# RWKV attention and a sentence-level expert layer: attention outputs summed transposed by 64x32 tiles, expert weights in halves, opening reordered

## The chip, the cores and the metric

One core of a Trainium2 chip. The metric is the device time of one launch in microseconds (us). A run is "fast" when it lies within 1.5% of the fastest run of the same kernel, else "slow"; comparisons below are of fast runs unless a sentence says otherwise. In the traces TensorE (PE in the profile, PEld for its weight loads) is granted either the full clock (1.00) or half of it (0.50); for a longer stretch the profile gives the mean.

## The reference

Four sequences of 768 positions, 8 heads of 48 columns. Attention keeps a 48x48 state a head; then each whole sequence is sent to one of 8 experts.

```python
for t in range(S):
    cur = einsum('bhd,bhe->bhde', u[None] * kt, vt)
    y[:, :, t] = einsum('bhd,bhde->bhe', rt, state + cur)
    state = w[None, :, :, None] * state + einsum('bhd,bhe->bhde', kt, vt)
x = y as (B, S, 384)
logits = x.mean(axis=1) @ w_gate            # one expert a sequence
e_idx = argmax(logits); gate_w = softmax(logits)[e_idx]
out = gate_w * (maximum(x @ w1[e_idx], 0) @ w2[e_idx])    # 384 -> 1024 -> 384
```

## The kernel before

The 768 positions of a sequence are three groups of 256, so there are 12 groups. A group is: scaled k and r (`kp`, `rp`), transposes of both, scores in two rounds masked by VectorE (`gt`), then y = scores x v, plus the bonus term u and the carried state. The suffixes `_x`, `_y` and names such as `kp`, `rp`, `vt` (v times the bonus) are tiles and helpers of the kernel; a "mode change" below is TensorE going from matmuls of one tile shape to those of another. `y` comes out with positions on the partitions, so ScalarE evicts it (`xn`), TensorE transposes it back, and ScalarE evicts it again into `xt`, which the expert layer reads. Sequence b's expert jobs (`hp`: 3 matmuls for the first layer; `op`: 4 for half of the second) are let into "slots" of the next sequence's groups, 8.5 a group in seven slots; the first gate must be known before the first job.

```python
def scores_v(g, j, first):                       # cut
    def y_mm(i):                                 # 32 a group: load 64x128, move 48 columns
        h, c = divmod(i, 2); p, a = divmod(h, 2)
        nc.tensor.matmul(out=yj[:, D * h : D * h + D],
            lhsT=gt[q, p // 2, a, p % 2, c, :], rhs=vb[q, c, h, :], ...)
    def s_mm(i):                                 # 16 a group: load 64x128, move 96 columns
        p, c = divmod(i, 2)
        nc.tensor.matmul(out=sp[:, 96 * p : 96 * p + 96],
            lhsT=kp[g % NR][qo, c, 2 * p : 2 * p + 2, :]..., rhs=vb[qo, c, 2 * p : 2 * p + 2, :]..., ...)
    for i in range(H):
        y_mm(2 * i)
        if with_state: s_mm(i)
        y_mm(2 * i + 1)

def add_bonus(g):                                # 4 matmuls a group, 384 columns each
    for j, c in ((0, 0), (1, 1), (0, 1), (1, 0)):
        nc.tensor.matmul(out=ys[g][j][64 * c : 64 * c + 64, 0:DM], lhsT=ident[q, q], rhs=vt[q, c, :], ...)

def backs(g):                                    # 6 transposes, 6 pooling matmuls, one 0.80 us copy
    ...
def mm1(b, w1, ht, ft, sb):
    for ct in range(NCT):
        nc.tensor.matmul(out=hp[:, 0:SB], lhsT=w1[:, ct, ft::NFT], ...)   # step 8 through w1
```

## Time and profile before

| | before |
|---|---|
| time, median of 3 runs (range) | 154.54 us (153.83 to 156.16) |
| span of the profile, mean clock | 152.6 us, 0.978 |
| first gate known; first expert job | 33.3; 45.0 us |
| last gate known | 120.3 us |
| matmuls (each has a weight load beside it) | 1951 |

How to read it: the opening (to 45 us) is a chain of waits; the loop (first job to last gate, 75.3 us) keeps TensorE full (busy 77.4 of the 78.5 us from 45 to 123.5); the tail (32.3 us) is expert jobs alone. The prediction below shows the rows. One view that I passed over belongs here, the DMA queues: queue, kind, packets, MB and share of the DMA engines' time.

```profile
q1 hardware_dynamic: 39460, 18.89, 42.9%
q0 software_dynamic: 1152, 6.29, 22.3%
q8 instruction: 15, 0.25, 0.6%
```

The last line is, by the view's name for it, the program itself on its way to an engine: 15 packets of 16 KB. At 0.6% of the DMA time it looks like nothing, and as bandwidth it is nothing.

### The profile page before, as it was taken

How to read it: one execution, taken by the hardware profiler on the slowest of the kernel's cores; microseconds unless marked ns; L12 is line 12 of the kernel's file. 1: busy time of each engine (PE TensorE's matmuls, PEld its weight loads, DVE VectorE, ACT ScalarE, POOL GpSimd, SP SyncE). 2: the span in 40 equal slices, each digit the busy share in tenths (PEclk: the TensorE clock that was granted, in tenths of full speed). 3: DMA queues.
4: the chain of work that ended last, by engine and by line, in shares of the span. 5: the costliest groups of instructions: out<-in, count | busy, mean ns of one | idle time of the engine just before them, and what ended most of it. 6: DMA issues, size and time to landing. Idle time of an engine off the chain costs nothing.

```text
span 152.6 us, 4539 instructions
## 1 busy us (share of the span) xinstructions
PE 139.5 (91%) x1951; PEld 97.9 (64%) x1951; DVE 74.4 (49%) x164; ACT 83.6 (55%) x144; POOL 68.5 (45%) x62
## 2 busy tenths in 40 slices
PE   6999877956989999999999999999999999999991
PEld 2266645644767878766677877666777765676560
DVE  7837796125465654754548456465562321121110
ACT  0976567351356766546476784563664543556231
POOL 4169659207976839289292862963021020000000
PEclk9999999995599999999999999999999999999999
DMA  2999998303999999999991000998020079960034
GB/s 59 301 322 321 279 268 226 99 0 92 227 215 297 249 312 269 293 214 210 215 376 48 4 0 4 153 195 267 22 93 4 0 111 208 161 247 0 0 126 185
DMA packets 41464, 25.47 MB, mean 167 GB/s; under 512 B 38755, under 2 KB 39012, under 8 KB 41444
## 3 DMA queue, kind: packets, MB, share of 16 engines
q1 hardware_dynamic: 39460, 18.89, 42.9%
q0 software_dynamic: 1152, 6.29, 22.3%
q8 instruction: 15, 0.25, 0.6%
q10 hardware_dynamic: 832, 0.00, 0.3%
q14 instruction: 5, 0.04, 0.1%
HBM read 26.76 MB, written 4.72 MB: 206 GB/s over the span
## 4 chain that ended last, share of the span: by engine, by line
PE 78%; DVE 10%; ACT 8%; issue 2%; DVEq 0%
PE op L503 21%; PE hp L483 21%; PE twp L236 7%; PE at L260 5%; DVE gt L268 5%; PE fill L113 5%; PE y L353 5%; ACT kr L246 4%; PE s L361 2%; PE xp L402 2%; ACT ht L490 2%; PE y L313 2%; PE y L323 2%; DVE ht L492 1%; DVE st L376 1%
## 5 line engine op out<-in xcount | busy, mean ns | idle before, releaser
L483 PE MATMUL hp<-xt,w 128*128 128x384 bf16 x192 | 41.4, 334 | 1.3 <-DVE lg L436 0.3
L503 PE MATMUL op<-w,ht 128*128 128x384 bf16 x192 | 34.9, 326 | 0.1
L246 ACT COPY kr<-twp 128x1024 bf16<-128x1024 bf16 x24 | 24.1, 1011 | 18.4 <-PE twp L236 18.4
L268 DVE TENSOR_TENSOR gt<-at,mask 128x1024 bf16<-128x1024 f32 x24 | 29.3, 1221 | 8.8 <-PE at L260 8.6
L490 ACT ACTIVATE ht<-hp 128x384 bf16<-128x384 f32 x48 | 23.4, 491 | 17.8 <-PE hp L483 17.1
L483 PEld LDWEIGHTS <-w 128*128 128x128 bf16 x192 | 25.0, 148 | 8.1 <-issue 4.4
L305 POOL TENSOR_TENSOR vt<-vb,tcol 128x768 bf16<-128x768 bf16 x11 | 16.3, 1477 | 25.4 <-DVE tcol L297 25.4
L503 PEld LDWEIGHTS <-ht 128*128 128x128 bf16 x192 | 17.3, 97 | 11.1 <-issue 0.8
L247 DVE TENSOR_TENSOR prod<-twp,kr 128x512 bf16<-128x512 bf16 x24 | 10.2, 424 | 27.8 <-ACT kr L246 27.8
L199 POOL TENSOR_TENSOR kp<-k,dk 128x768 bf16<-128x768 f32 x11 | 20.0, 1816 | 1.4 <-DMA k<-in_k_dram 1.4
L199 POOL TENSOR_TENSOR rp<-r,dr 128x768 bf16<-128x768 f32 x11 | 20.0, 1820 | 0.0
L510 ACT ACTIVATE ob<-op,gw 128x384 f32<-128x384 f32 x16 | 9.3, 581 | 13.2 <-PE op L503 12.9
L113 PE MATMUL fill<-zero 128*128 128x512 bf16 (+1 forms) x45 | 14.5, 430 | 1.9 <-DVE zero L85 1.3
L353 PEld LDWEIGHTS <-gt 64*128 64x128 bf16 x384 | 11.5, 94 | 5.0 <-issue 3.9
L492 DVE TENSOR_SCALAR ht<-hp 128x384 bf16<-128x384 f32 x16 | 8.9, 554 | 11.7 <-PE hp L483 11.5
L353 PE MATMUL y<-vb,gt 64*128 64x48 bf16 x384 | 14.1, 182 | 0.4 <-ACT xn L389 0.4
L260 PE MATMUL at<-kr 48*64 48x128 bf16 x384 | 10.5, 229 | 3.6 <-ACT kr L246 1.7
L389 ACT CAST xn<-y 128x384 bf16<-128x384 f32 x24 | 11.1, 480 | 4.1 <-PE y L323 3.5
L462 POOL DMA_DIRECT2D w<-in_moe_w_dram x4 | 2.5, 623 | 22.5 <-DVE gw L452 7.8
L260 PEld LDWEIGHTS <-kr 48*64 48x64 bf16 x384 | 7.0, 110 | 8.2 <-issue 6.2
L410 ACT COPY xt<-xp 128x768 bf16<-128x768 bf16 x12 | 9.6, 798 | 4.3 <-PE xp L402 4.3
L361 PE MATMUL s<-vb,kp 64*128 64x96 bf16 x160 | 10.5, 208 | 0.4 <-DVE st L376 0.4
(73 smaller groups left out, 155.6 us busy)
## 6 DMA issues: line engine op xcount, KB each, us to landing
w<-in_moe_w_dram POOLq DMA_DIRECT2D x8, 768.0 KB, 10.2
k<-in_k_dram SPq DMA_DIRECT2D x12, 384.0 KB, 5.1
r<-in_r_dram SPq DMA_DIRECT2D x12, 384.0 KB, 5.8
v<-in_v_dram SPq DMA_DIRECT2D x12, 384.0 KB, 5.7
out_dram<-ob SPq DMA_DIRECT2D x11, 384.0 KB, 5.6
out_dram<-ob SPq DMA_DIRECT2D x2, 192.0 KB, 1.9
wuT<-in_w_dram ACTq DMA_DIRECT2D x2, 0.8 KB, 3.6
wuT<-in_u_dram ACTq DMA_DIRECT2D x2, 0.8 KB, 4.1
```

Source lines behind the costliest of these rows:

```text
L113: nc.tensor.matmul(out=fills[-1][:, 0:cols], lhsT=zero[:, 0:128], rhs=zero[:, 0:cols], start=True, stop=True)
L199: eng.tensor_mul(dst[:, cs, :, 0:D].rearrange("q c h d -> q h c d"), src[:, :, cs, :], dec[:, :, cs, :])
L246: nc.scalar.copy(kts[g][:, :, :, c, :], tw)
L260: nc.tensor.matmul(out=at[64 * j : 64 * j + 64, a, pp, cs, :], lhsT=kt[q, p, j, cs, :], rhs=rt[q, p, j].rearrange("q c i -> q (c i)"), sta ...
L268: nc.vector.tensor_mul(gts[g][:, rnd].rearrange("q a p c t -> q (a p) c t"), at.rearrange("q a p c t -> q (a p) c t"), mask.rearrange("q n ...
L305: nc.gpsimd.tensor_mul(vt, vbs[g].rearrange("q c h d -> q (c h) d"), tcol.to_broadcast([128, 2 * H, D]))
L353: nc.tensor.matmul(out=yj[:, D * h : D * h + D], lhsT=gt[q, p // 2, a, p % 2, c, :], rhs=vb[q, c, h, :], start=(first and i == 0), stop=(c ...
L361: nc.tensor.matmul(out=sp[:, 96 * p : 96 * p + 96], lhsT=kp[g % NR][qo, c, 2 * p : 2 * p + 2, :].rearrange("s a b -> s (a b)"), rhs=vb[qo, ...
L389: nc.scalar.copy(xns[g][:, j, :], ys[g][j][:, 0:DM])
L483: nc.tensor.matmul(out=hp[:, 0:SB], lhsT=w1[:, ct, ft::NFT], rhs=xts[b][:, ct, SB * sb : SB * sb + SB], start=(ct == 0), stop=(ct == NCT - 1),
L490: nc.scalar.activation(out=o, in_=hp[:, 0:SB], func=ACT.Relu)
L503: nc.tensor.matmul(out=op[:, 0:DM], lhsT=ht[:, ft, 128 * si : 128 * si + 128], rhs=w2[:, ft, :], start=(ft == 0), stop=(ft == NFT - 1),)
```

## The change

Its intent: sum y already transposed (channels on the partitions), so that the two evictions, the back transposes and the pooling matmuls go; pack the sums into 64x32 tiles and scores and state into 64x64 tiles, so that several run side by side (in the trace before, four score matmuls on four 64x64 tiles start within 10 ns, at 89.54 us); fetch each expert's w1 as two halves, whose weight slices step by 4 elements in place of 8; and reorder the opening around a shorter path to the first gate. The core of the diff, cut:

```diff
-    wrow = const.tile([1, DM], FP32, tag="wrow", name="wrow")
-    nc.sync.dma_start(out=wrow, in_=w.rearrange("(o h) d -> o (h d)", o=1))
+    wbc = const.tile([128, DM], FP32, tag="wbc", name="wbc")
+    nc.sync.dma_start(out=wbc, in_=w.rearrange("h d -> (h d)").partition_broadcast(128))
+    load(0, "kr")
+    load(1, "kr")
...
+        def mm(h, c, u):                                   # y: 64 a group, load 64x32, move 128
+            nc.tensor.matmul(
+                out=y_slice(ys[g][j], G), lhsT=vb[q, c, o : o + 32],
+                rhs=gts[g][q, p // 2, a, p % 2, c, :], ...
+        def mm(p, u):                                      # carried state: 32 a group
+            nc.tensor.matmul(
+                out=y_slice(ys[g][j], G), lhsT=sts[g, j][q, p, 32 * u : 32 * u + 32], ...
+        def mm(G, c):                                      # bonus: 48 a group, load 64x32, move 64
+            nc.tensor.matmul(
+                out=y_slice(ys[g][j], G)[:, 64 * c : 64 * c + 64],
+                lhsT=vt[q, c, 32 * G : 32 * G + 32], rhs=ident[q, q], ...
+        def mm(h, c):                                      # state: 32 a group, 64x64
+            nc.tensor.matmul(
+                out=s_ps[g // NB][64 * a : 64 * a + 64, 64 * p : 64 * p + 64],
+                lhsT=kp[g % NR][q, c, h, :], rhs=vb[q, c, window(h) : window(h) + 64], ...
...
+    def part_y(g):
+        together(row0, row1)                # y, bonus, carried state: up to 112 matmuls in turn
+        nc.tensor.drain()
+        together(inter_mms(g, 0, 1), inter_mms(g, 1, 0))
+        together(state_mms(g, 1))
...
-        w1 = wpool.tile([128, NCT, F], BF16, tag="w1", name=f"w1_{b}")
+        for fh in range(2):
+            t = wpool.tile([128, NCT, HF], BF16, tag=f"w1_{fh}", name=f"w1_{b}_{fh}")
...
     gate(0)
     weights(0)
     gate_weight(0)
...
+    bonus(3)
+    prep_k(4)                               # GpSimd's k and r of group 4, now behind the weights
+    prep_r(4)
...
+        slot()
+        acc[1] = True                       # jobs let in from the third slot of group 3, not the sixth
```

## The prediction

> **What bounds the kernel now.** I read the page's engine rows and slices first, then the chain that ended last in order of time, then the groups of instructions.
>
> ```profile
> PE 139.5 (91%) x1951; PEld 97.9 (64%) x1951; DVE 74.4 (49%) x164; ACT 83.6 (55%) x144; POOL 68.5 (45%) x62
> ...
> PE   6999877956989999999999999999999999999991
> ...
> PEclk9999999995599999999999999999999999999999
> ```
>
> TensorE is the only engine near its limit, and the clock row shows where it is not: slices 9 and 10 (34 to 42 us) are half speed. The stretches view says the same in three stages:
>
> ```profile
> 45.00:123.50 78.50, 77.40 (x1217) 58.19 (x1210) 42.57 (x90) 47.98 (x84) 41.07 (x32) 1.00 0.64 160
> 123.50:152.60 29.10, 25.24 (x145) 16.10 (x142) 4.70 (x8) 11.01 (x21) 0.00 (x0) 1.00 0.52 134
> 35.00:45.00 10.00, 8.62 (x168) 6.29 (x167) 5.87 (x9) 3.60 (x6) 9.62 (x8) 0.69 0.88 187
> ```
>
> From 45 to 123.5 us TensorE is busy 77.4 of 78.5 us: nine attention groups and expert jobs share it, and nothing else matters there. Before 45 us the kernel is a chain of waits through all engines; after 123.5 us only expert jobs are left. The chain, at the points that bound the stages:
>
> ```profile
> 33.28 0.18 DVE top L438
> ...
> 35.06 0.67 PE at L260 x12
> ...
> 45.11 0.64 PE hp L483 x3
> ...
> 75.32 0.45 PE twp L236 x8
> ...
> 84.66 0.45 PE twp L236 x8
> ...
> 94.39 0.45 PE twp L236 x8
> ...
> 123.53 7.82 PE op L503 x48
> ...
> 134.45 1.21 PE hp L483 x6
> ```
>
> The first gate is known at 33.3 us, the first expert job runs at 45.1, and one group's transposes return every 9.3 to 9.7 us. The slot rate puts 8.5 expert jobs into a group.
>
> [...]The old w1 slice steps 8 bf16[...]; the new one steps 4[...]. [...]step 8 loads in 148 ns, step 3 in 104, contiguous in 97.
>
> ```profile
> L483 PEld LDWEIGHTS <-w 128*128 128x128 bf16 x192 | 25.0, 148 | 8.1 <-issue 4.4
> L503 PEld LDWEIGHTS <-ht 128*128 128x128 bf16 x192 | 17.3, 97 | 11.1 <-issue 0.8
> ...
> L402 PEld LDWEIGHTS <-xn 128*128 128x128 bf16 x72 | 5.0, 104 | 1.7 <-ACT xn L389 0.9
> ```
>
> [...]The score matmuls show it: four on four 64x64 tiles start within 10 ns, the next four 56 ns later[...].
> [...]The trace has about 0.10 us between the end of one mode's stream and the next mode's first matmul (scores to expert job at 89.80 to 89.89)[...].
>
> **The change part by part, in the steady loop.** From the starts in the trace, one middle group costs TensorE before: transposes 16 x 55.7 ns = 0.89; scores 2 x 0.35 = 0.70; bonus column 0.20; y with state 2 x 0.50 = 1.00; the state's share of y 8 x 66 ns = 0.53; bonus into y 0.29; back transposes 6 x 55.7 = 0.33; pooling 6 x 26 = 0.16; carried state 0.26. Sum 4.36 us. Jobs: an hp job is 3 x 183 ns = 0.55, an op half job 4 x 167 = 0.67, so 16 and 12 of them average 0.60, times 8.5 = 5.1. Together 9.5, which is the period seen.
>
> After, matmuls grow from 1951 to about 3160. I count tiles: a tile is held 56 ns by 128 columns and 29 ns by 64[...], so a run of four that names a tile twice takes two turns. Part x: 16 y matmuls of one row tile in the column order 0,1,3,0 then 1,2,0,1: 0.40. Part y: the longer row has 32 y in the same order (0.79), 24 bonus (0.18) and 8 carried (0.15): 1.1[...]. The drain: last matmul's latency of 0.2[...], 0.3. Behind it 16 matmuls, 0.17. State: 2 x 16 matmuls of 64 columns on two tiles, 0.24 each. Scores stay in the state's mode: 0.25 + 0.25. Transposes 0.89, carried 0.11, bonus column 0.20, logits 6 x 26 ns = 0.16. Mode changes 6 x 0.10 = 0.6. Sum 4.9 us (5.4 with slower issue). So a group costs TensorE 0.55 us more, not less: 64x32 tiles would be cheap if the eight were used evenly, but the order hits one tile twice in four, and 176 matmuls stand where 72 stood. Over eight and a half groups: +4.7 us.
>
> Given back: step-4 weights. In a long stream the 143 ns load hides under 162 ns of matmul; it shows only after short matmuls, where the second hp matmul starts 220 ns after the first instead of 162. That is about 58 ns in some 40 stretches, 2.3 us. In the tail hp jobs run at 0.63 us because two PSUM banks wait for their eviction (0.49 to 0.57), so nothing is gained there. The gate: six fp32 passes of 127 ns become two, 0.5 us at each of three gates in the loop, 1.5 us. ScalarE loses one 0.80 us copy a group, and VectorE some 0.3, but neither is the bound, so that is worth nothing in the loop. Net of the loop: about +1 us.
>
> **The opening.** The w broadcast puts 0.2 MB ahead of the inputs; at about 0.3 MB/us k and r land 0.6 us later, and r set the first transposes before. Gained back: VectorE makes one of the two kr copies, so the first masked scores start at about 11.2 us (11.4 before). Then I walked the new order with the measured durations: vt on VectorE to 15.1, part y of group 0 to 16.75, then st, prod, and scores of group 1 at 17.7 (16.65 before), 19.4; the logits of group 0 wait for the gate constants that GpSimd makes behind a 1.48 us vt, to 21.5; part x, transposes, part y of group 1 to 25.8; scores of group 2 at 26.75 and 28.45 (21.1 and 24.6 before). Here the transposed sum pays: from the last score mask to the gate's logits there are 4.8 us instead of 8.7, without xn, back transposes and pooling. The first gate comes at about 33.2 us, where it is now (33.1).
>
> From the gate to the first job: before, 12 us, in which kp of group 4 was already done. After, GpSimd has weights (1.8), then vt of group 3 (1.48), kp and rp of group 4 (1.82 each) in that order, and vt waits for the bonus column behind exps, vb (0.84), kr (1.01), prod (0.42), the second transposes, kr, prod, and a 1.22 us mask: about 7 us after the gate. So rp of group 4 ends some 12 us after the gate; the transposes of group 4 wait for it, then scores, part x and the second transposes, which wait for a kr copy. First job about 15.5 us after the gate, near 49 us, 4 us later than now, although half of w1 should have landed 7.3 us after the gate (issue at +2.05, first packet 2.8 later, 2.3 for a half). Part y of group 3 and more stands behind it than before (+1.8), while three more slots per the first group take four jobs out of the tail, at nearly no gain.
>
> Sum: 152.6 span +4 (first job) +1.8 (more of group 3 left) +1 (loop) -0.5 (tail) = 158.9 us, and the time is 1.8 above the span: 160.7. I do not take it whole: the walk stacks waits, each of which I may have put too late, and nobody writes a change of this size to lose 6 us. I go to 157.
>
> **Rivals.** First, the opening is shorter: if the waits I stacked overlap and the first job is bound by the half of w1 alone, it starts 7.3 us after a gate at 31 to 33 us, so at 39 to 41, and the loop costs the same: 152.6 - 5 + 1.8 + 0.5 = 150 span, about 151. The halves and the earlier start of the jobs speak for it; the order of GpSimd's work (weights, vt, kp, rp) against. Second, tiles pack better than my count: if the column conflicts cost nothing, part y is 0.6 and a group 4.2 us, 6 us less in all, 147 to 151.[...] Third, issue or the load of 64-column weights becomes the bound[...]: +0.7 us a group, 163 to 166. Fourth, ScalarE was the hidden bound and its saved 0.80 us a group shortens the period: 48 us busy of 78.5 speaks against it.
>
> **Range and chances.** My count says slower, the rivals that mend the opening or the packing say faster, and they are independent of each other. I give 157 us, 148.5 to 165, faster by over 2% (under 151.5) 0.27, within 2% 0.33, slower (over 157.6) 0.40.
>
> **What would show it.** The period of the transposes in the loop: 9.5 to 9.9 if the count is right, under 9 if tiles pack. Part y from first to last matmul: 1.5 to 1.6 us with its drain. The w load at 104 to 110 ns. The first gate at 32 to 35 us and the first hp at 47 to 50; GpSimd's rp as what the transposes of group 4 wait for. A first hp at 40 us would break the sum, and so would a group's attention under 4.3 us.

The sum: 4.9 us for a group, 158.9 us for the span, 160.7 us for the time, taken down to 157. Of the drain's 0.3 us only the 0.2 of a matmul's record is from the trace (state and y records are 0.18 to 0.21); the other 0.1 was the author's assumption. The 5.4 us of a group "with slower issue", and with it the third rival's +0.7, stood on a slower issue rate that no trace had shown. The 29 ns for 64 columns are the author's estimate, between the starts in the trace for 48 columns (25 ns apart, L353) and for 96 (43, L361). That a run of four which names a tile twice takes two turns, and that step 4 loads faster than step 8, were assumptions when they were written (in the changed kernel the last of part x's y matmuls start in pairs 52 to 54 ns apart, 69.57 to 69.74 us); the 104 to 110 ns given for the load lie near the 104 of step 3. Against the second rival the trace has only that y matmuls alone start 26 ns apart (16 from 87.45 us), and y and state matmuls in turn 17 (24 from 85.70).

## The result, and the profile after

The changed kernel is correct and takes **192.66 us** (191.32 to 194.07, 4 fast runs) against 154.56 (153.83 to 156.16, 4 runs). The ratio of fast runs is 1.2486, 95% interval 1.2367 to 1.2605. That is 38 us slower, far outside the range of 148.5 to 165.

Busy rows and clock row of the changed kernel:

```profile
PE 150.5 (78%) x3157; PEld 99.6 (52%) x3159; DVE 71.9 (37%) x154; ACT 72.8 (38%) x126; POOL 75.7 (39%) x75
...
PE   7487449683269699989859689996696998769992
...
PEclk9999655566555999999988978999799999978999
```

TensorE is busy 78% of the span where it was busy 91%, in a kernel that gave it more instructions; no other engine is fuller than before. The clock row has half-speed digits through slices 5 to 13, and dips later, where the kernel before had two. So nothing is a busy bound here: TensorE waits. From the start times in the two traces:

| stage | before | after | difference |
|---|---|---|---|
| start to first gate | 33.3 | 43.1 | +9.9 |
| first gate to first expert job | 11.8 | 16.2 | +4.5 |
| first job to last gate (the loop) | 75.3 | 101.4 | +26.2 |
| last gate to end | 32.3 | 31.5 | -0.8 |
| span | 152.6 | 192.3 | +39.7 |

What does it wait for? The chain of waits of the changed kernel (start, length, what):

```profile
1.77 6.74 DMA r<-in_r_dram
...
18.49 2.96 issue
...
51.80 1.79 POOL kp L199
53.59 1.77 POOL rp L199
55.40 0.60 PE twp L235 x4
...
65.50 1.16 issue
...
96.98 1.91 issue
...
109.71 1.25 issue
...
133.82 2.43 issue
...
146.34 1.64 issue
...
162.47 7.19 DMA w<-in_moe_w_dram
```

"Issue" is time in which the engine waited for nothing that the profile shows. It is 10% of the chain. Read alone, these lines say only that TensorE stood still, once in most groups but not in all, and in different places of a group. The stretches between them say why. Columns: stretch, length, then busy us and instruction count of PE, PEld and the other engines, clock and DMA:

```profile
66.00:85.20 19.20, 17.89 (x511) 13.04 (x511) 9.61 (x17) 10.28 (x18) 10.95 (x8) 1.00 0.38 91
85.20:98.00 12.80, 10.76 (x255) 7.11 (x255) 6.27 (x18) 4.92 (x9) 8.13 (x7) 1.00 1.04 215
98.00:110.30 12.30, 9.88 (x256) 6.68 (x255) 4.18 (x8) 5.52 (x10) 5.79 (x4) 0.86 0.84 198
110.30:135.00 24.70, 21.70 (x511) 14.70 (x511) 11.33 (x26) 10.32 (x18) 13.91 (x11) 0.93 0.34 65
135.00:147.00 12.00, 9.99 (x255) 6.91 (x256) 3.93 (x8) 4.70 (x8) 1.47 (x1) 0.86 0.38 105
```

I cut the time at six idle spells (65.5, 84.9, 97.0, 109.3, 133.2 and 146.3 us). Matmuls plus weight loads between them are 1022, 510, 511, 1022 and 511: within a record or two lost, multiples of 512, whatever the work between them. TensorE stops at every so many *instructions*. And the instruction queue of the changed kernel has

```profile
q8 instruction: 24, 0.39, 0.8%
```

24 packets of 16 KB for 6316 TensorE instructions, 263 each (before: 15 for 3902, 260 each). With the counts above, a packet is a block of 256. In the trace the idle spells stand at TensorE's instructions 447, 959, 1983, 3007, 3519, 4031, 5055 and 5567, each one short of 192 + 256k. The spell at 133 us in detail, the DMA queues in the stretch 130.5 to 133.9 us:

```profile
q0 software_dynamic: 584, 0.65, 115.8%
```

and in 133.9 to 135.3 us:

```profile
q0 software_dynamic: 75, 0.22, 85.2%
q1 hardware_dynamic: 23, 0.07, 14.9%
q8 instruction: 1, 0.02, 4.3%
```

By the records, TensorE entered the block from instruction 4800 at 130.41 us and had used it up at 133.20, because part y, its drain and the next state and scores are about 320 instructions in a burst. The fetch of the following block ran from 134.05 to 135.01 and the first instruction from it started at 136.24, 3.05 us after the last. Over the whole trace such a fetch starts 0.4 to 3.7 us after a block is entered (once 0.1 before) and takes 0.9 to 1.5, and after a spell TensorE resumes 1.2 to 1.6 us after its end. The blocks ahead of the eight spells were used up in 1.8 to 4.1 us, and the first instruction of the next one started 3.0 to 6.0 us after they were entered. The shortest blocks with no such spell behind them lasted 3.0 us (72.3 to 75.4) and 3.2 (119.9 to 123.2), the next 5.3. In the kernel before, blocks lasted 6.5 us and more, and no such spell exists. The eight spells sum to 13 us.

How late the fetch starts goes with the data on the DMA engines. Nine of the 24 fetches started more than 1.5 us after their block was entered, and in that time the engines were 78% busy or more with inputs or weights, each time; in only three of the other fifteen were they busy. No run changed that traffic alone, so it is a reading of the trace, not a shown cause.

Behind most of the longer spells the clock fell as well. In the 2.96 us spell at 18.5 us the clock fell, at 20.9; after those at 97.0 (1.91 us), 109.3 (1.61) and 133.2 (3.05) it was half from 99.4 to 102.8, 113.1 to 116.5 and 136.9 to 140.4: 3.4 us each time. After the 1.64 us at 146.3 it stayed full. The changed kernel has 52 us of its span at half clock, 38 of them ahead of 62 us, the kernel before 7. What sets the clock was not shown; spells of 1.6 and 1.9 us were followed by its fall. At half clock the same work took twice as long (`hp` matmuls start 320 ns apart instead of 163), so from that and the 3.4 us I estimate that a spell of 2 us with 3.4 us of half clock behind it costs 3.7.

### The profile page after: what moved, and what is told of

It is laid out like the page before. It is cut to its first block, busy times and chain, and to the rows that moved or that the text cites. A ratio compares the mean times of both kernels' runs of the same rounds, so it can differ in the third digit from the quotient of the medians.

```text
span 192.3 us, 6945 instructions
## 1 busy us (share of the span) xinstructions
PE 150.5 (78%) x3157; PEld 99.6 (52%) x3159; DVE 71.9 (37%) x154; ACT 72.8 (38%) x126; POOL 75.7 (39%) x75
## 4 chain that ended last, share of the span: by engine, by line
PE 64%; issue 10%; DVE 9%; DMA 7%; ACT 5%; POOL 3%; SPq 0%; POOLq 0%; DVEq 0%
PE hp L537 18%; PE op L557 13%; PE y L335 7%; PE twp L235 7%; DVE gt L274 4%; PE at L266 4%; DMA w<-in_moe_w_dram 4%; PE y L354 4%; DMA r<-in_r_dram 4%; PE s L385 3%; PE y L369 2%; PE fill L120 2%; ACT kr L249 2%; ACT ht L544 1%; PE s L468 1%
## 5 line engine op out<-in xcount | busy, mean ns | idle before, releaser
L305 POOL TENSOR_TENSOR vt<-vb,tcol 128x768 bf16<-128x768 bf16 x11 | 16.2, 1473 | 60.5 <-DVE tcol L304 60.5
L537 PEld LDWEIGHTS <-w 128*128 128x128 bf16 x192 | 20.6, 120 | 18.8 <-issue 8.8
L460 ACT CAST xt<-y 128x384 bf16<-128x384 f32 x23 | 10.2, 480 | 23.0 <-PE y L354 15.4
L235 PE MATMUL twp<-ident,kp 128*128 128x128 bf16 x96 | 11.6, 256 | 8.1 <-POOL kp L199 4.1
L335 PE MATMUL y<-gt,vb 64*32 64x128 bf16 x768 | 17.7, 237 | 0.3 <-DVE vt L301 0.3
L266 PE MATMUL at<-kr 64*64 64x128 bf16 x384 | 12.7, 247 | 4.8 <-DVE gt L274 2.5
L335 PEld LDWEIGHTS <-vb 64*32 64x32 bf16 x768 | 13.3, 97 | 4.1 <-issue 3.5
L235 PEld LDWEIGHTS <-kp 128*128 128x128 bf16 x96 | 8.7, 118 | 12.3 <-issue 4.5
L514 POOL DMA_DIRECT2D w<-in_moe_w_dram x8 | 6.4, 805 | 20.7 <-DVE gw L501 20.7
L369 PE MATMUL y<-ident,vt 64*32 64x64 bf16 x576 | 11.5, 202 | 3.0 <-issue 3.0
L266 PEld LDWEIGHTS <-kr 64*64 64x64 bf16 x384 | 8.6, 120 | 9.6 <-issue 8.5
## 6 DMA issues: line engine op xcount, KB each, us to landing
w<-in_moe_w_dram POOLq DMA_DIRECT2D x4, 768.0 KB, 12.7
```

The costliest lines, as they stand in the source:

```text
L235: nc.tensor.transpose(out=twp[:, o + p, :], in_=src[:, c, 2 * p : 2 * p + 2, :].rearrange("s a b -> s (a b)"), identity=ident,)
L266: nc.tensor.matmul(out=at[64 * j : 64 * j + 64, a, pp, cs, :], lhsT=kt[q, p, j, cs, :], rhs=rt[q, p, j].rearrange("q c i -> q (c i)"), sta ...
L305: nc.gpsimd.tensor_mul(vt, vb, tcol.to_broadcast([128, 2 * H, D]))
L335: nc.tensor.matmul(out=y_slice(ys[g][j], G), lhsT=vb[q, c, o : o + 32], rhs=gts[g][q, p // 2, a, p % 2, c, :], start=first(g, j, G), stop= ...
L369: nc.tensor.matmul(out=y_slice(ys[g][j], G)[:, 64 * c : 64 * c + 64], lhsT=vt[q, c, 32 * G : 32 * G + 32], rhs=ident[q, q], start=first(g, ...
L460: nc.scalar.copy(xv[:, :, :, j, :], src)
```

## The experiments

Two theories. **Supply** (called F): TensorE runs out of fetched instructions, so the number of instructions, and how fast a stretch uses them, sets the loss. **Tiles** (T): the small tiles cost array time, drains and mode changes, more than I counted. Beside these, the opening has its own rivals. Sixteen kernels ran, each beside runs of the kernel before on the same chip (medians 154.5 to 155.8).

**Is it array time?** Same instructions, a quarter of the columns moved by the y matmuls (wrong result):

```diff
-                out=y_slice(ys[g][j], G), lhsT=vb[q, c, o : o + 32],
-                rhs=gts[g][q, p // 2, a, p % 2, c, :],
+                out=y_slice(ys[g][j], G)[:, 0:32], lhsT=vb[q, c, o : o + 32],
+                rhs=gts[g][q, p // 2, a, p % 2, c, 0:32],
```

> The changed kernel with the y matmuls moving 32 columns instead of 128 (a wrong result on purpose): the same instructions, less array time. F: the same gaps at the same instruction numbers, 189 to 193 us. T: 64 y matmuls a group at a quarter of the columns save up to 0.5 us a group, 185 to 188 us.

191.89 us (191.06 to 193.17). Leaving out three quarters of the y columns gains under 1 us, and the idle spells stayed at the same instruction numbers (447, 1983, 3007, 3519, 4031, 5055, 5567). Together they grew from 13.2 to 16.4 us: array time that was saved was spent waiting for the same blocks. So array time is not the bound here; what it would cost without the waits, this run can't say.

**Is it a wait for the bonus operand?** The bonus matmuls read v in place of v times the bonus, so that nothing waits for GpSimd's product (wrong):

```diff
-            vt = vts[g].rearrange("q (c h) d -> q c (h d)", c=2)
+            vt = vbp[g % NR].rearrange("q c h d -> q c (h d)")
```

> The changed kernel with the bonus matmuls reading v itself instead of v times the bonus (wrong result on purpose): all instructions stay, only the wait for the product on GpSimd goes. If the 19 us that the run without bonus matmuls gained came from instructions (F), this one stays at 189 to 193 us; if they came from the wait that went with them, 172 to 178.

192.83 us (191.1 to 193.6): nothing.

**Fewer instructions.** The 48 bonus matmuls of a group left out (wrong):

```diff
-        for c in range(2):
+        for c in range(0):
```

> The changed kernel without the 48 bonus matmuls of a group (a wrong result on purpose): 576 matmuls, 1152 instructions or 4.5 blocks fewer. F: fewer blocks to wait for and a shorter burst, 176 to 185 us. T: 48 matmuls at 8 to 12 ns in twelve groups are 5 to 7 us of array time, 186 to 188 us. The gaps that are left stand at block boundaries of the new count in F, at the same places of the program in T.

173.26 us median (169.91 to 174.06; by the 1.5% rule only the lowest, the profiled one, counts as fast). 19 us for 576 matmuls which, at the 0.18 us a group that I had counted, are 2 us of array time. Twenty blocks were fetched in place of 24. Better than both theories said. It takes instructions and their array time away together, so by itself it does not tell the theories apart.

**More instructions, in the kernel before.** This is the pair that tells the two apart without the changed kernel's other parts: idle matmuls of zeros added behind each loop group's y, either 112 of 64x32 tiles (224 instructions) or 18 of 128x128 with 128 columns (36 instructions).

```diff
+        for i in range(56):                      # dense: two row tiles each
+            for r in range(2):
+                nc.tensor.matmul(out=ys[g][r][c : c + 32, DM : DM + 64],
+                    lhsT=zero[q, 0:32], rhs=zero[q, 0:64], start=False, ...)
+        for i in range(18):                      # wide, in the other kernel
+                nc.tensor.matmul(out=ys[g][i % 2][:, DM : DM + 128],
+                    lhsT=zero[:, 0:128], rhs=zero[:, 0:128], start=False, ...)
```

> The kernel before with 112 small idle matmuls (64x32 tiles, 64 columns of zeros, into unused columns) in one burst in each of the nine loop groups: 2016 instructions more, some 1 us of array time a group. F: the burst runs through most of a block faster than the next arrives, so 9 us of array time plus 1 to 2.5 us of waiting at a block boundary in most groups, 170 to 182 us, with idle gaps at instruction numbers 192 + 256k. T: array time alone, 163 to 166 us.

> The kernel before with 18 idle matmuls of 128 columns on the whole array in the same place: the same array time of 1 us a group from 36 instructions instead of 224. F and T alike: 163 to 166 us, no gaps at block boundaries. It is the control of the run with 112 small ones.

Both give right results. Dense: 174.84 us, the median of two fast runs (172.62, 173.36) and two slow ones. Wide: 164.37 us (163.85 to 166.05), ratio 1.0595 (1.0514 to 1.0676). The fast runs are 8.3 us apart (means 172.99 and 164.66). Chain of waits of the dense kernel, then its stretches between these spells:

```profile
53.78 1.53 issue
81.37 1.11 issue
111.99 2.87 issue
124.87 0.88 issue
```

```profile
55.00:82.00 27.00, 25.93 (x639) 19.61 (x640) 13.12 (x27) 14.22 (x25) 12.90 (x11) 1.00 0.93 222
82.00:113.50 31.50, 29.30 (x768) 22.77 (x768) 14.64 (x32) 17.52 (x30) 18.50 (x14) 1.00 0.30 73
113.50:125.30 11.80, 10.01 (x256) 6.95 (x256) 4.92 (x8) 4.37 (x6) 1.47 (x1) 1.00 0.36 98
```

1279, 1536 and 512 instructions: 5, 6 and 2 blocks. The kernel before, which never stood at a block boundary, does so as soon as a burst of small matmuls is put into it, and its spells in the loop sum to 6.9 us (those of the chain and one of 0.5 at 49.7); the wide kernel has none. The queue of the dense kernel fetched 23 blocks, that of the wide one 16, which are again the TensorE instructions (5915 and 4223) over 256:

```profile
q8 instruction: 23, 0.38, 0.8%
q8 instruction: 16, 0.26, 0.6%
```

I had sized both for about 1 us of array a group (18 x 56 ns wide; 112 x 8.5 ns dense), and the traces bear it out: where no spell falls into it, the dense burst takes 0.89 us and the wide one 0.96. The dense loop is 7.1 us longer than the wide one, 6.9 of it spells. Supply is shown. The clock stays full through the dense kernel's loop, its 2.87 us spell included, so half clock did not follow there.

**Spreading the burst.** The same instructions, with an expert slot between y and bonus of part y, and the next scores behind a slot:

```diff
+        together(row0[:32], row1[:16])
+        mid()
+        together(row0[32:], row1[16:])
```

> The changed kernel, with an expert slot moved into part y of every loop group (between the y matmuls and the bonus) and the scores of the next group put behind another slot: the same instructions, less dense. Theory F (TensorE runs out of instructions: a block of 256 arrives 3 to 6 us after the block before it began, and the gaps stand at instruction numbers 448 + 512k): the loop's gaps of about 10 us shrink by half or more, and the half-clock spells behind them, so 180 to 187 us. Theory T (the added matmuls and mode changes themselves cost the time): one mode change more in each of nine groups, so 192 to 196 us.

A miss: 192.16 us (190.85 to 192.74). Some spells went or shrank (those at 1983, 3007, 4031 and 5567), but 2.03 us at 3519 and 2.73 at 5055 stayed, and the new order gave five of the logits waits of 0.45 to 0.71 us, and another mode change a group. The loop's spells fell from 9.9 to 5.5 us and its half clock from 12.7 to 6.8, yet the loop got only 2.0 us shorter. Where the rest went is open beyond these waits: removing spells was not worth their whole length here.

**The weights alone, in the kernel before.** As halves, and then w1 whole but read in steps of 4 within each half:

```diff
-                out=hp[:, 0:SB], lhsT=w1[:, ct, ft::NFT],
+                out=hp[:, 0:SB], lhsT=w1[ft // 4][:, ct, ft % 4 :: 4],                       # halves
+                out=hp[:, 0:SB], lhsT=w1[:, ct, 512 * (ft // 4) : 512 * (ft // 4 + 1)][:, ft % 4 :: 4],  # step 4
```

> The kernel before with the expert weights in halves alone (w1 slices of step 4 instead of 8, w2 ordered to fit). The prediction's reading: weight loads fall from 148 to about 105 ns, about 2 us off, 152 to 153 us. Rival: the halves' transfers, cut into 1 KB pieces, land later than the whole did (7.3 us from issue to landing), and take it back: 154 to 157 us.

> The kernel before with w1 brought whole as before but read with step 4 (f split in two within the tile, w2 ordered to fit): the stride without the halved transfers. If the stride is worth what the prediction counted, 2 us off: 152 to 153.5 us; if the halves' 0.7% loss was the stride's doing, 155 to 156.

Halves: 155.83 us (154.91 to 157.64), ratio 1.0072 (1.0023 to 1.0122). Step 4 with one whole transfer: **153.95 us** (153.5 to 154.5), ratio 0.9891 (0.9842 to 0.9939), the fastest kernel, though within 2%. Both count as the same as before at 2%; the runs before in the second lot lie between 154.21 and 156.53, so fastest against fastest step 4 gains 0.7 us. In both the load of w falls from 148 ns to 116; the row of the second:

```profile
L483 PEld LDWEIGHTS <-w 128*128 128x128 bf16 x192 | 19.2, 116 | 11.8 <-issue 5.1
```

So the slice step is worth about 1 to 2 us and the halves give it back: in the changed kernel, which has the same halves, GpSimd spends about 0.8 us on each of three issues where it spent 0.5 to 0.6 on each of two, and half of w1 takes 7.1 us from issue to landing where the whole took 7.3. The chain of the halves kernel shows the issues ahead of `rp`, for which the transposes wait:

```profile
36.29 0.74 POOL w L471
37.05 1.82 POOL rp L199
...
38.92 0.61 PE twp L236 x4
```

Its gate to first job is 13.9 us against 11.8 before, its loop 74.7 against 75.3.

**The opening.** Three edits to the changed kernel, alone and together: w as one row spread by a matmul (as before); GpSimd's `prep_k(4)`, `prep_r(4)` ahead of the gate; 14 wide idle matmuls so that TensorE isn't idle where it waits.

```diff
+    nc.sync.dma_start(out=wrow, in_=w.rearrange("(o h) d -> o (h d)", o=1))     # row
+    prep_k(4); prep_r(4)          # ahead of logits(1) and gate(0)              # early k, r
-    fill(1, 512)
+    fill(7, 512)                  # behind part_x(0)                            # pad
+    fill(8, 512)                  # ahead of logits(0)                          # pad
```

> The changed kernel, with w brought in as one row and spread over the partitions by a matmul, as in the kernel before, in place of the 128-partition DMA that stands ahead of r and k in the changed kernel. If that DMA holds the inputs back (chain of waits: r 6.74 us from issue), the first r/k work starts 1.5 to 2 us earlier, the first gate comes at 40 to 41 us instead of 43.1, and the time is 188 to 191 us. If the opening is set by the fetch gap and the half clock alone, the gate stays within 1 us and the time at 192 to 193 us.

> The changed kernel, with GpSimd's k and r products of group 4 put ahead of the logits and the gate instead of behind the expert weights. Gate to first expert job, 16.4 us in the changed kernel with 3.6 us of these products and a 4.06 us wait of TensorE for them in its chain, should fall to 8 to 11 us if these products set it, and the time to 184 to 188 us. If the weights' own landing sets the first job, it stays at 14 us or more and the time at 190 to 193 us.

> The changed kernel with seven wide idle matmuls in place of one after the first part x, and eight more ahead of the first logits: only 14 more instructions pairs, but TensorE is at work where it would have idled. If the 20.5 us at half clock in the opening follow from the idle spells, the opening's clock rises from 0.55 to 0.75 or more, the gate comes 2 to 6 us earlier and the time is 186 to 190 us. If the clock has another cause, the gate comes 1 to 3 us later and the time is 193 to 196 us.

> The three edits of this batch together: w as one row, the products of group 4 ahead of the gate, and the wide idle matmuls. If the opening's losses (gate 9.8 us later, first job 14.4 us later than before) are these three, the first expert job comes at 46 to 51 us instead of 59.4 and the time is 178 to 184 us, still well above the kernel before, since the loop's own loss (about 22 us between the first job and the last gate) is untouched. If the losses are those of instruction supply everywhere, it stays above 188 us.

The row: 191.25 us median, but 189.49 and 189.72 in its fast runs, 3 us less than the changed kernel's median; the first gate came at 38.5 us in place of 43.1, better than the 40 to 41 expected. The first transposes of r, whose transfer ends the first wait of the changed kernel's chain, start at 8.1 us in place of 9.2: the DMA of w ahead of the inputs did hold them back.

Early k and r: 191.64 us median, one fast run of 187.57. Its profiled run was slow, so I use of it only distances. Gate to first job fell from 16.2 to 10.3 us, as expected; yet the second gate came at 89.2 us, where the changed kernel has 88.3. Its chain shows where the six microseconds went:

```profile
52.80 0.97 PE hp L537 x6
...
57.60 2.31 issue
...
72.93 1.92 issue
```

These two spells, at instructions 1983 and 2495, were 1.16 us and none in the changed kernel. The block ahead of the first was entered nearly 8 us earlier (54.0 us), while weights were arriving, and the fetch behind it started 3.47 us later, where it had started 2.18. Half clock follows them, too (59.1 to 69.3 us). Part of that may be the slow run's own.

Padding: 195.82 us (193.73 to 199.88), a miss. The half clock of the opening stayed (22.8 to 33.0 and 36.4 to 60.3, 34 us, where the changed kernel has 38), and the spells kept their numbers (447, 958, 1982, 2494, 3518, 5054, 5566, the last digit off by a lost record) although 28 instructions more stood ahead of most of them: the number decides, not the work at that place. All three together: 186.07 us (184.68 to 187.0), short of the 178 to 184 expected, with the pads' 3 us in it.

**Fewer instructions with a right result.** If supply is the cause, the cheapest repair is to take the bonus, a product with the identity, by 64x128 tiles: 12 matmuls a group in place of 48, 72 instructions fewer, the same columns for each bank. They run behind the y and carried matmuls, which adds a mode change (about 0.10 us by the trace before, scores to expert job at 89.80 to 89.89 us).

```diff
-                out=y_slice(ys[g][j], G)[:, 64 * c : 64 * c + 64],
-                lhsT=vt[q, c, 32 * G : 32 * G + 32], rhs=ident[q, q],
+                out=ys[g][j][:, o + 64 * c : o + 64 * c + 64],
+                lhsT=vt[q, c, o : o + 128], rhs=ident[q, q],                # o = 128 * ct
```

> The changed kernel with the bonus added by 12 matmuls of 64x128 tiles a group in place of 48 of 64x32: the same sums, a right result, the same columns moved per bank, 72 TensorE instructions a group fewer (a matmul and its load are two), and one mode change a group more. If the supply of instructions limits (a_nobonus, 96 fewer, came to 170 to 174 us), the time is 174 to 182 us, three instruction fetches fewer than 24, and the idle spells at multiples of 256 instructions shrink to under 8 us from 13. If array time or mode changes limit, it stays within 190 to 194 us, or is slower by the mode change (0.1 us a group, 1 us).

> The same with two of the earlier edits to the opening, w as one row and group 4's products ahead of the gate (the idle matmuls stay out, they cost 3 us alone). If the early first job was given back before only because the loop ran into the instruction supply (new gaps of 2.3 and 1.9 us at TensorE instructions 1983 and 2495), the opening's gain of 8 to 11 us should now stand: 166 to 173 us. If it is given back again, 174 us or more. In both cases it stays above the kernel before (154.5).

Both hits. The wide bonus alone: 176.64 us (175.1 to 177.66), correct, 16 us less for 432 matmuls that no longer run. Its clock row and instruction queue:

```profile
PEclk9969955555555699999999999999999999999999
```

```profile
q8 instruction: 21, 0.34, 0.8%
```

From slice 15 the clock is full to the end, and of the boundary spells only 2.43 us at 449 is left. The loop fell from 101.4 to 86.7 us. A pause of 1.69 us ahead of 92.5 us looks like one more, six instructions short of a boundary, but the chain has a weight transfer there, and its block had been fetched by 89.4 us:

```profile
85.29 7.15 DMA w<-in_moe_w_dram
```

The row and the early k and r go on top of this. With both it is 168.2 us (167.83 to 170.64), ratio 1.0825: now the opening's gain stands (8.4 us), where without the wider bonus the early k and r had gained the second gate nothing.

**What is left.** That kernel's loop is 88.3 us against 75.3, with boundary spells of about 0.4 us alone. Its chain has two waits for an expert's weights, in the loop and behind the last gate:

```profile
75.17 7.14 DMA w<-in_moe_w_dram
...
136.79 7.19 DMA w<-in_moe_w_dram
```

The change lets expert jobs in three slots earlier, so fewer are left at a gate to cover the next weights: 5 at the second gate and 10 at the last, where the old place leaves 8.6 and 13.6. Undone alone, and with 7.5 jobs a group on top:

```diff
-        acc[1] = True                 # behind the second slot
+        acc[1] = True                 # behind the fifth slot
-    RATE = 8.5 / 7
+    RATE = 7.5 / 7                    # second kernel only
```

> The kernel with the wide bonus and the two edits to the opening, with the first expert jobs let in three slots later, as in the kernel before, so that 3.6 more jobs are left at each gate to cover the new expert's weights (5 left at the second gate and 10 at the last become 8.6 and 13.6; its chain of waits has 7.1 us of weight transfer at 75 us and 7.2 at 137 us). If the weights' wait is what keeps its loop 13 us above that of the kernel before, the time falls to 162 to 166 us from 168.2. If the jobs taken out of the third group only leave TensorE idle there, it stays at 167 to 171 us.

> The same with 7.5 expert jobs a group in place of 8.5, so that 11, 16 and 22 jobs are left at the gates. If the wait for weights is the bound, it falls further, to 160 to 165 us; if the attention of a group, with its waits among the engines, takes longer than the jobs in it can fill, it rises to 169 us or more.

165.63 us (165.05 to 166.97), ratio 1.07 (1.0656 to 1.0744), and no weight transfer in the chain any more: a hit. With 7.5 jobs 167.46 us (166.96 to 168.06), a miss between its two cases: the loop gets shorter by less than the tail gets longer. The first of them is the best form of the changed kernel that I found, and still 11 us behind the kernel before. Of its span's 12.4 us over the kernel before, 4.5 lie ahead of the first gate, 2.3 between gate and first job, 7.4 in the loop, and the tail is 1.8 shorter.

## Why the prediction was wrong

The step that failed is the one from the group to the loop, from "So a group costs TensorE 0.55 us more" to "+4.7 us" and "about +1 us" net: it priced 1200 added matmuls by the time that they hold the array, and took for granted that TensorE has the instructions to hand. In its place the loop took 26.2 us more, of which 9.9 are pauses for instruction blocks and about 6.3 half clock. The direction was right, as its likeliest outcome, for another reason than the one given. The third rival came near it and named issue, but at 0.7 us a group and on a rate that no trace had shown; no step asked how instructions get to the engine.

- **The array count was near.** In a group of the changed kernel with no spell in it (67.7 to 76.8 us) the attention took 4.99 us of TensorE, in one before with the same 24 first-layer matmuls (75.2 to 84.5 us) 4.42: 0.57 more, where 0.55 was predicted. The 112 matmuls of part y started within 1.03 us (104 within 0.93 in a sequence's first group), under the 1.1 counted, and the drain took 0.32, near the 0.3 of the sum. On one tile 64-column state matmuls start 32 ns apart, not the 29 counted. The rival that tiles pack better, with 4.2 us a group, falls.
- **The loop** took 26.2 us more, not 1. My sum of what is known: 9.9 us of spells at block boundaries, 6.3 for 12.7 us at half clock, 4.8 for the count above over 8.5 groups, 1.8 for the larger rest of group 3 as predicted: 22.8. The remaining 3.4 is not assigned, and more than that if the step-4 weights and the gate gave back what was predicted. The run with the spread burst warns that such terms don't simply add. In the best repaired kernel 7.4 us are left in the loop, near the 6.6 of the last two terms, though its bonus and job order differ.
- **The first gate** came at 43.1 us, not 33.2. "At about 0.3 MB/us k and r land 0.6 us later" was too small: the first transposes of r started at 9.2 us against 8.1, the first masking of scores at 13.4 against 11.4 before and 11.2 predicted, and with w as a row the gate came 4.7 us sooner. The chain puts the rest down to a 2.96 us spell at a block boundary, half clock behind it, and 2.1 us of waiting for the gate constants, which I had in the walk; no run separates these, and the idle matmuls that were tried did not bring the clock back there.
- **Gate to first job** was predicted at 15.5 us and took 16.2, with `rp` of group 4 as the last wait, as its chain shows: right, and confirmed by moving these products. The rival that the halves alone bound it falls.
- **Step-4 weights**: 120 ns after, and 116 alone, against 104 to 110 predicted: step 4 did not reach the 97 ns of the contiguous load (`ht`). The 2.3 us given for it is near the truth for the step (1.7 us, the difference of the two ratios, 1.0 and 0.9891, times 154.6) but not for the halves that the change used to get there (+1.1 us in place of a gain).
- **Earlier jobs** "take four jobs out of the tail, at nearly no gain": a loss. They are what covers the weights (2.6 us by the run that undid it, in the repaired kernel).
- **The chances**: 0.40 for slower was the largest, but the range ended at 165, because every rival was made of work on engines and of waits that the profile names.

## What to carry to other kernels

Count TensorE's instructions (a matmul and its load are two) beside its columns: in the changed kernel the next 256 came to start 3.0 to 3.6 us after a block was entered, or 4.8 to 6.0 at the spells where inputs or weights kept the DMA engines 78% busy or more, and a stretch that used up 256 in less than that stood still. Half clock followed four of its five such pauses of 1.6 us or more, and not the 2.87 us one of the dense kernel. Before you split matmuls into small tiles, look at the instruction queue's packets and at "issue" in the chain, and cut the stretches at such pauses: if the counts between them are multiples of 256 within a record or two (here 1022, 510, 511, 1022 and 511), it is supply; a pause at a boundary with a transfer in the chain may still be the transfer. An earlier start was worth nothing here while a later limit waited (gate to first job 10.3 us in place of 16.2, the second gate at 89.2 in place of 88.3), and work pulled forward may be what covered a transfer (2.6 us here).
